# A written-out order of 1,538 steps replaced by one of 1,570, on a fused attention and filter kernel

## The chip, the cores and the metric

The kernel runs on one core of one Trainium2 chip. The metric is the device time of one execution in microseconds (us). Of the kernel before, three executions were timed: 292.82, 293.58 and 296.74 us, median 293.58 us. The profile is of one execution on that core.

The core has a matrix engine (PE, with its weight loads shown as PEld), a vector engine (DVE), a scalar engine (ACT), a general engine (POOL) and a sequencer for transfers (SP). Each engine works through its own list of instructions in order. POOL and SP also issue transfers: those of POOL run in one transfer queue (q0, "software_dynamic" in the profile), those of SP in another (q1, "hardware_dynamic").

## The reference

The computation is a feature-map attention for 8 batches and 8 heads over 576 positions, whose output goes through a gated circular convolution:

```python
def phi(x):
    proj = np.einsum('bhsd,df->bhsf', x, w_phi)              # 64 -> 128 features
    proj = proj - np.max(np.abs(proj), axis=-1, keepdims=True)
    return np.concatenate([np.exp(proj), np.exp(-proj)], axis=-1)
q_p, k_p = phi(q), phi(k)
kv  = np.einsum('bhsf,bhsd->bhfd', k_p, v)
z   = np.sum(k_p, axis=2)
num = np.einsum('bhsf,bhfd->bhsd', q_p, kv)
den = np.einsum('bhsf,bhf->bhs', q_p, z)[..., None] + 1e-06
x   = (num / den).transpose(0, 2, 1, 3).reshape(8, 576, 512)

proj = x @ w_proj                                            # 512 -> 3 * 512
x1, x2, x3 = thirds of proj
x2_conv = irfft(rfft(x2, n=576) * rfft(filter, n=576), n=576)
out = (x1 * x2_conv * x3) @ w_out
```

Inputs and output are float32. q, k and v have the shape (8, 8, 576, 64), the output (8, 576, 512).

## The kernel before

**Stages.** Each of the eight batches b goes through the same chain. Its parts are named by short words, which are also the method names of the class `Kernel`:

- `load` and `loadh` (lines 596 and 602) fetch a batch, or half a batch, of q, k or v through POOL's queue as bf16. `trh` (line 608) transposes half a batch of q or k by a transfer that SP issues. For batch 0 the transposes run on PE instead (`pt`, line 618), with a copy out of PSUM (`pte`).
- `Pk`, `Qn` (and `Pkt`, `Qnt` for the leftover positions) multiply by w_phi on PE (lines 636, 643, 651). `maxk`, `maxq` take the maxima of the absolute values on DVE (line 716). `ex` takes the exponentials of k on ACT (line 698). `mhi`, `mlo`, `trm`, `trme` prepare the maxima of q as a transposed row, and `Pq` (lines 670 and 676) projects q with those maxima subtracted; `ex` takes its exponentials too.
- `em` (ACT, line 752) and `vs` (POOL, line 758) scale v. `KV` (line 773), `KVe`, `NE` (line 787), `rc` and `xn` (lines 801 and 806) make the normalised attention output. `trx` (line 825) transposes it by a transfer of SP, `ptx` on PE.
- `f1`, `f2` (lines 854 and 860, sums and differences, on POOL or DVE), `Ft` and `Fs` (PE, lines 869 and 876) are the forward transform; `Fe` and `Xl` copy it out. `X2` (line 895), `Y1` (lines 900 and 905, DVE) and `m3` (line 909) project and multiply by the filter's transform. `I` (line 970), `Ie` (ACT, line 988), `Ip`, `Im` (DVE, line 991) are the inverse transform. `X1`, `X3` (line 917), `X1e`, `tm` and `ym` (line 1005) give the gate, `O` (line 1016), `Oe` and `st` (line 1040) the output.

**Start.** The transform matrices are made on the chip: `gi_part`, `gi_col`, `gi_fr`, `gi_nr`, `gi_back` write index numbers on POOL (iota), `cols_a`, `cols_b` and `ang` make angles of them (DVE, one `ang` on ACT), `frac` takes them into range (DVE), `sin` takes sines (ACT). The filter is fetched by nine transfers of SP (`fl_loadt`, `fl_load`), `fa` (POOL, line 495) makes its sums and differences `fs`, then `rev`, `fb`, `Ff`, `Ffe`, `H` and `He` make its transform. `wz` multiplies zeros on PE and feeds nothing. `exz` loads ACT's table for exponentials.

**What sets the order.** Nothing is scheduled by a tool here. The string `PLAN` lists all steps, and `run` calls them one by one; the order in which the calls of one engine stand is that engine's list. A word such as `Pk,1,0@2` is the step, its arguments (batch, part) and its PSUM bank; `KVe,ACT,1,0@4` names the engine that does the copy. Buffers go round as `RING` says (line 22): a step that writes a buffer waits until its last reader is done.

**Space in the start.** `fs`, the filter's sums, lies in the tile `turn`, which also holds the angles. So `fa` waits until the sines have read them:

```python
self.fs = self.turn.rearrange("p a x -> p (a x)")[:, 0:2048].rearrange(
    "p (a x) -> p a x", a=4)
```

The index numbers `fr` and `nr` have tiles of their own.

Of the kernel before, what the change touches and what calls it, by code (L numbers as in the profile page):

```python
# [30 lines left out]
gz,DVE sin,9 fz,DVE cz,DVE,0 loadh,q,0,0 gi_nr cz,DVE,1 gi_part gi_col cols_a cols_b cols_h  # L31
loadh,k,0,0 gi_fr ang,DVE,2 wz,23@0 wz,30@1 wz,31@0 wz,32@1 wz,33@0 ang,ACT,3 fl_loadt ident frac,3
frac,2 pt,q,0,0,0@0 pt,q,0,0,1@1 ang,DVE,1 wz,0@2 wz,34@3 wz,35@2 pt,k,0,0,0@3 ang,DVE,0
pt,k,0,0,1@2 frac,1 pte,DVE,q,0,0,1@1 zeros frac,0 fl_load,0,0 fl_load,2,1 ft,DVE fl_load,0,1
w_load,phi w_phi gi_back wz,18@1 back pte,DVE,k,0,0,0@3 Pk,0,0@4 loadh,q,0,1 sin,3 pte,ACT,q,0,0,0@0
pte,DVE,k,0,0,1@2 loadh,k,0,1 sin,2 sin,1 one Qn,0,1@0 Pk,0,1@2 pt,q,0,1,0@6 wz,27@7 sin,0 wz,14@7
fl_load,1,1 pt,k,0,1,1@7 exz ex,k,m,0,1@2 maxk,0,0@4 maxq,0,1@0 fl_load,3,1 fl_load,2,0 ex,k,p,0,0@4
pt,k,0,1,0@0 load,v,0 ex,k,m,0,0@4 pt,q,0,1,1@1 load,k,1 fl_load,3,0 maxk,0,1@2 pte,ACT,k,0,1,1@7
fl_load,1,0 pte,DVE,q,0,1,0@6 pte,ACT,k,0,1,0@0 Qn,0,0@4 pte,ACT,q,0,1,1@1 load,q,1 fa,POOL,0
maxq,0,0@4 Pkt,0@6 Qn,0,3@0 trh,k,1,0 maxkt,0@6 ex,k,p,0,1@2 wz,24@4 wz,17@2 trh,q,1,0 Qnt,0@4  # L40
maxq,0,3@0 fa,POOL,1 em,p,0,0 exkt,p,0@6 Pk,0,2@0 exkt,m,0@6 Qn,0,2@2 ex,k,p,0,2@0 maxqt,0@4
Pk,0,3@6 maxq,0,2@2 em,m,0,0 ex,k,m,0,3@6 w_load,proj,2 mhi,0 ex,k,p,0,3@6 rev@4 maxk,0,2@0
vs,POOL,p,0,0 mlo,POOL,0 vs,POOL,m,0,0 ex,k,m,0,2@0 trm,0@2 trme,DVE,0@2 Pq,0,0@2 ex,q,p,0,0@2
Pq,0,1@0 maxk,0,3@6 fb,0@4 em,m,0,1 em,p,0,1 vs,POOL,p,0,1 fb,1@4 wz,11@6 wz,9@7 KV,0,0@6
ex,q,p,0,1@0 ex,q,m,0,1@0 ex,q,m,0,0@2 Pq,0,3@4 Pq,0,2@0 ex,q,m,0,3@4 KVe,DVE,0,0@6 vs,POOL,m,0,1
NE,0,0@6 rc,0,0@6 NE,0,1@2 xn,0,0@6 trh,q,1,1 ex,q,p,0,3@4 Ff,2@6 Pk,1,1@4 rc,0,1@2 xn,0,1@2
f1,POOL,0,0,0 maxk,1,1@4 ex,q,p,0,2@0 Ffe,ACT,2@6 KV,0,1@2 Qn,1,0@6 ex,q,m,0,2@0 wz,5@0
# [1049 lines left out]
```

## Time and profile before

| | us |
|---|---|
| median of three executions | 293.58 |
| span of the profiled execution | 291.2 |
| PE busy | 274.0 (94%) |
| DVE busy | 252.3 (87%) |
| POOL busy | 228.5 (78%) |
| ACT busy | 221.9 (76%) |
| transfers: q1 (SP) / q0 (POOL), share of 16 transfer engines | 48.0% / 36.6% |

For the profiled execution the span, from the first to the last instruction, is the time that is given; the median of the timed executions is 2.4 us more. Busy time counts each matmul with its whole passage, and matmuls overlap, so a PE that is shown as busy need not be at its highest pace. "Idle before" in a row is the time in which the engine stood still ahead of that instruction, with what ended it.

### The profile page before, as it was taken

The numbers are of one execution on the slowest core, as the hardware profiler recorded it, in microseconds if no ns is written. First come the engines' busy times: TensorE is split into PE (matmuls) and PEld (weight loads), VectorE is DVE, ScalarE is ACT, GpSimd is POOL, SyncE is SP. The second block draws the span as 40 slices with busy tenths as digits, with TensorE's granted clock in tenths as the row PEclk, the third lists the DMA queues.
The fourth block names the chain that finished last, engine by engine and source line by source line (L and its number), as shares of the span: only waits on it lengthen the run. The fifth ranks groups of instructions, "written<-read, shape, count | busy, mean of one in ns | idle before, by whom it ended". The sixth has DMA issues, their size and how long they took to land.

```text
span 291.2 us, 10275 instructions
## 1 busy us (share of the span) xinstructions
PE 274.0 (94%) x4336; PEld 194.8 (67%) x4336; DVE 252.3 (87%) x438; ACT 221.9 (76%) x367; POOL 228.5 (78%) x187
## 2 busy tenths in 40 slices
...
GB/s 140 230 207 175 144 204 165 139 175 181 143 192 177 163 204 159 153 119 165 122 111 156 197 169 114 163 135 191 99 14 93 84 36 2 34 108 54 69 130 184
DMA packets 72319, 40.07 MB, mean 138 GB/s; under 512 B 52496, under 2 KB 67216, under 8 KB 72272
## 3 DMA queue, kind: packets, MB, share of 16 engines
q1 hardware_dynamic: 57136, 22.62, 48.0%
q0 software_dynamic: 14816, 16.25, 36.6%
...
q10 hardware_dynamic: 320, 0.52, 0.7%
q14 instruction: 13, 0.11, 0.1%
HBM read 33.75 MB, written 9.44 MB: 148 GB/s over the span
## 4 chain that ended last, share of the span: by engine, by line
PE 71%; DVE 3%; ACT 2%; issue 1%; DVEq 0%; ACTq 0%
PE ps L917 17%; PE ps L895 11%; PE ps L1016 10%; PE ps L970 8%; PE ps L773 5%; PE ps L787 4%; PE ps L876 3%; PE ps L926 2%; PE ps L670 2%; PE ps L636 2%; PE ps L643 2%; PE ps L676 2%; PE ps L869 2%; DVE mq L716 1%; PE ps L796 1%
## 5 line engine op out<-in xcount | busy, mean ns | idle before, releaser
L917 PE MATMUL ps<-xT,wproj 128*128 128x256 bf16 x512 | 64.0, 273 | 0.2 <-DMA wproj<-in_moe_w_proj_dram 0.2
L917 PEld LDWEIGHTS <-wproj 128*128 128x128 bf16 x512 | 48.1, 98 | 9.0 <-DMA wproj<-in_moe_w_proj_dram 0.4
L1005 POOL TENSOR_TENSOR yT<-cv,x1s 128x576 bf16<-128x576 f32 x31 | 39.4, 1279 | 15.6 <-ACT es L988 7.7
L716 DVE TENSOR_REDUCE mq<-ps 128x8 f32<-128x1024 f32 (+1 forms) x40 | 43.7, 1112 | 3.5 <-PE ps L643 1.5
L716 DVE TENSOR_REDUCE mk<-ps 128x8 f32<-128x1024 f32 (+1 forms) x40 | 44.1, 1112 | 2.9 <-PE ps L636 1.6
L758 POOL TENSOR_TENSOR vm<-vn,vm 128x1152 bf16<-128x1152 bf16 x16 | 34.3, 2152 | 7.4 <-ACT vm L752 7.4
L758 POOL TENSOR_TENSOR vp<-vn,vp 128x1152 bf16<-128x1152 bf16 x16 | 34.4, 2155 | 4.6 <-ACT vp L752 4.5
L698 ACT ACTIVATE Eqp<-ps 128x1024 bf16<-128x1024 f32 x32 | 32.9, 1038 | 6.1 <-PE ps L676 6.0
L854 POOL TENSOR_TENSOR SD<-xn 128x512 bf16<-128x512 bf16 x28 | 31.9, 1153 | 6.2 <-DVE xn L806 4.7
L1016 PE MATMUL ps<-wout,yT 128*128 128x512 bf16 x140 | 34.8, 379 | 0.1
L860 POOL TENSOR_TENSOR xf<-SD 128x512 bf16<-128x512 bf16 x26 | 29.7, 1155 | 6.4 <-DVE SD L854 5.9
L698 ACT ACTIVATE Ekp<-ps 128x1024 bf16<-128x1024 f32 x32 | 33.2, 1036 | 1.1 <-PE ps L636 0.7
L698 ACT ACTIVATE Eqm<-ps 128x1024 bf16<-128x1024 f32 x32 | 32.6, 1037 | 1.6 <-PE ps L676 0.8
L698 ACT ACTIVATE Ekm<-ps 128x1024 bf16<-128x1024 f32 x32 | 33.1, 1033 | 0.8 <-PE ps L636 0.7
L895 PE MATMUL ps<-wproj,XF 128*128 128x512 bf16 x128 | 31.6, 379 | 0.3 <-ACT x1s L298 0.3
L991 DVE TENSOR_TENSOR cv<-es,ps 128x288 f32<-128x288 f32 x64 | 26.3, 445 | 5.7 <-ACT es L988 4.4
L909 POOL TENSOR_TENSOR T<-T,T 128x1024 bf16<-128x1024 bf16 x14 | 29.6, 2127 | 1.7 <-DVE r L801 0.8
L970 PE MATMUL ps<-inv,T 128*128 128x288 bf16 x192 | 28.1, 286 | 0.7 <-DVE mq L716 0.4
L958 DVE TENSOR_TENSOR x1s<-ps,x1s 128x512 bf16<-128x512 f32 x32 | 21.8, 685 | 2.5 <-PE ps L917 1.1
L298 ACT COPY o<-ps 128x512 f32<-128x512 f32 x20 | 11.8, 600 | 14.4 <-PE ps L1016 12.0
L806 DVE TENSOR_TENSOR xn<-ps,r 128x512 bf16<-128x512 f32 x32 | 21.9, 689 | 0.9
L298 ACT CAST x1s<-ps 128x512 bf16<-128x512 f32 (+1 forms) x33 | 17.4, 540 | 6.7 <-PE ps L917 3.2
...
## 6 DMA issues: line engine op xcount, KB each, us to landing
...
```

The costliest lines, as they stand in the source:

```text
L298: self.nc.scalar.copy(dst, src)
L698: self.nc.scalar.activation(e, p, AF.Exp, bias=0.0, scale=1.0 if g == "p" else -1.0)
L716: self.nc.vector.tensor_reduce(out=out, in_=src, axis=AX.X, op=ALU.max, apply_absolute_value=True)
L758: self.eng(eng).tensor_tensor(out=t[:, :, :, 0:64], in0=self.at("vn", b)[:, 2 * X:2 * X + 2], in1=t[:, :, :, 64:65].to_broadcast([128, 2, ...
L854: self.eng(eng).tensor_tensor(out=o[:, :, 2 * i:2 * i + 2, :], in0=x[:, :, 0:2, :], in1=x[:, :, 2:4, :], op=ALU.subtract if i else ALU.add)
L860: self.eng(eng).tensor_tensor(out=o[:, :, 2 * i:2 * i + 2, :], in0=x[:, :, 0:4:2, :], in1=x[:, :, 1:4:2, :], op=ALU.subtract if i else ALU ...
L895: self.mm(self.pb(0), l, w[:, kt, 512:1024], start=(kt == 0), stop=(kt == 3))
L909: self.eng(eng).tensor_tensor(out=Y, in0=Y, in1=self.at(f"T{2 * e + 1}", b), op=ALU.add)
L917: self.mm(o[:, d], w[:, kt, f0 + 128 * m:f0 + 128 * m + 128], y[:, 1, ::-1, ::-1] if d else y[:, 0], start=(kt == 0), stop=(kt == 3))
L970: self.mm(self.pb(e, 0, 288), l, inv[:, 2 * e + i if i < 2 else 4 + e, :], start=(i == 0), stop=(i == 2))
L1005: self.eng(eng).tensor_tensor(out=self.at("yT", b)[:, m, 0:SEQ], in0=self.turn_of("cv", (b, m)).rearrange("p x h t -> p (x h t)"), in1=sel ...
L1016: self.mm(self.pb(0), y[:, kt, 128 * c:128 * c + 128], w[:, kt, :], start=(kt == 0), stop=(kt == 3))
```

## The change

Four things change.

1. **The table of steps.** All of `PLAN` is replaced. The steps are the same apart from the inverse transform (point 4), but they stand in another order, with other PSUM banks, and some are given to another engine:

| step | before | after |
|---|---|---|
| `Fe` | 25 ACT, 7 DVE | 22 ACT, 10 DVE |
| `Ffe` | 4 ACT | 2 ACT, 2 DVE |
| `Xl` | 7 ACT, 1 DVE | 1 ACT, 7 DVE |
| `Oe` | 20 ACT, 15 DVE | 24 ACT, 11 DVE |
| `X1e` and `X1te` | 33 ACT, 7 DVE | 31 ACT, 9 DVE |
| `pte` | 4 ACT, 4 DVE | 2 ACT, 6 DVE |
| `yt` | 3 ACT, 1 DVE | 2 ACT, 2 DVE |
| `m3` | 14 POOL, 2 DVE | 12 POOL, 4 DVE |
| `ym` | 31 POOL, 1 DVE | 29 POOL, 3 DVE |
| `f2` | 26 POOL, 6 DVE | 24 POOL, 8 DVE |

`f1`, `KVe`, `trme`, `ptxe` and `He` keep their counts but change places: two `f1` of batch 1 go from POOL to DVE, and two of batch 5 go back.

2. **Index steps first.** In POOL's list the index steps stand ahead of the first `loadh`, and the first load is of k, where it was of q.

POOL's first instructions before, from the end of the program's prologue to the second load (nr, part, idx and raw are index numbers, qn and kn the inputs q and k of batch 0):

```order
L602 DMA qn_76<-in_q_dram 128x2x576
L342 ISA
L342 IOTA nr 128x256
L344 IOTA nr 128x32
L322 IOTA part 128x1
L323 IOTA idx 128x128
L388 IOTA raw 128x4
L389 IOTA raw 128x1
L390 MEMSET raw 1x1
L602 DMA kn_78<-in_k_dram 128x2x576
```

The same place after, to the first load (fsx is the new tile, which now holds fr and nr):

```order
L319 IOTA part 128x1
L320 IOTA idx 128x128
L385 IOTA raw 128x4
L386 IOTA raw 128x1
L387 MEMSET raw 1x1
L329 IOTA fsx 128x288
L330 IOTA fsx 128x2x16
L332 IOTA fsx 128x2x128
L334 MEMSET fsx 128x1
L339 IOTA fsx 128x256
L341 IOTA fsx 128x32
L599 DMA kn_78<-in_k_dram 128x2x576
```

Eleven index instructions now stand ahead of the first load, the four on `fr` among them, which came behind the second load.

3. **Filter sums in their own space.** A new tile `fsx` holds `fs`; `fr` and `nr` lie in its first 864 columns. `turn` holds angles alone. `fa` so waits for the readers of `fr` and `nr`, no longer for the sines.

POOL's list around `fa` before (line 495; vn is v, mh the prepared maxima of q, wproj the projection's weights):

```order
L596 DMA vn_80<-in_v_dram 128x4x576
L596 DMA kn_79<-in_k_dram 128x4x576
L596 DMA qn_77<-in_q_dram 128x4x576
L495 TENSOR_TENSOR turn<-fl 128x1024 x2
L586 DMA wproj_65<-in_moe_w_proj_dram 128x4x512
L758 TENSOR_TENSOR vp_105<-vn_80,vp_105 128x18x64
L740 TENSOR_TENSOR mh_90<-mq_88,mh_90 128x2x18
```

And after (line 492):

```order
L593 DMA vn_80<-in_v_dram 128x4x576
L593 DMA kn_79<-in_k_dram 128x4x576
L492 TENSOR_TENSOR fsx<-fl 128x1024 x2
L593 DMA qn_77<-in_q_dram 128x4x576
L755 TENSOR_TENSOR vp_105<-vn_80,vp_105 128x18x64
L737 TENSOR_TENSOR mh_90<-mq_88,mh_90 128x2x18
L755 TENSOR_TENSOR vm_119<-vn_80,vm_119 128x18x64
```

The load of q of batch 1 moved from ahead of the two sums to behind them, and the first weight load of `w_proj` left this place for one further on.

DVE's list before, at its first reductions (kT and qT are the transposed inputs, mk and mq the maxima):

```order
L593 CAST wphi_62<-phi 128x128
L501 TENSOR_SCALAR bk<-idx_277 128x128
L300 COPY kT_84<-ps 128x640
L300 COPY kT_84<-ps 128x512
L353 TENSOR_TENSOR onex<-ident_63 128x36
L354 SCALAR_TENSOR_TENSOR one_64<-onex 128x18
L716 TENSOR_REDUCE mk_86<-ps 128x2x4
L716 TENSOR_REDUCE mq_88<-ps 128x2x4
L716 TENSOR_REDUCE mk_86<-ps 128x2x4
L300 COPY qT_82<-ps 128x640
L716 TENSOR_REDUCE mq_88<-ps 128x2x4
```

And after:

```order
L590 CAST wphi_62<-phi 128x128
L498 TENSOR_SCALAR bk<-idx_258 128x128
L297 COPY kT_84<-ps 128x512
L713 TENSOR_REDUCE mk_86<-ps 128x2x4
L297 COPY qT_82<-ps 128x640
L297 COPY qT_82<-ps 128x512
L305 MEMSET mh_90 128x64
L305 MEMSET mh_91 128x64
L713 TENSOR_REDUCE mk_86<-ps 128x2x4
L297 COPY kT_84<-ps 128x512
L713 TENSOR_REDUCE mq_88<-ps 128x2x4
```

One copy stands ahead of the first reduction now, where two copies and the two instructions of `one` did; further copies come between the reductions.

4. **Inverse leftovers apart.** `I` (six matmuls, each over 128 rows) is gone. In its place stand `Is` (four matmuls, the main rows) and one of two forms for the leftover rows: `It` (two matmuls over 64 rows each, 15 times) or `Iz` (two matmuls over 128 rows, 17 times). Main and leftover rows may come in either order: `opens` remembers which of the two was called first, and that one starts the sum in PSUM. `Ft` and `Fs` are handled in the same way.

The last lines of the two tables, and the code:

```diff
-Oh,7,4,0@5 Oh,7,4,1@7 st,SP,7,2,1 st,ACT,7,0,0 Oeh,DVE,7,4,0@5 sth,SP,7,4,0 Oeh,DVE,7,4,1@7
-sth,SP,7,4,1
+sth,SP,7,4,0 st,ACT,7,1,1 Oh,7,4,1@2 Oe,DVE,7,2@4 st,SP,7,2,1 Oeh,DVE,7,4,1@2 st,SP,7,0,1 sth,SP,7,4,1
+st,ACT,7,2,0
...
     def gi_fr(self):
-        g, s = self.nc.gpsimd, self.scr
-        self.fr = s.tile([128, 2, 2, 144], FP32, name="fr")
+        g = self.nc.gpsimd
+        self.fr = self.fsx[:, 0:576].rearrange("p (a b x) -> p a b x", a=2, b=2)
...
     def gi_nr(self):
-        g, s = self.nc.gpsimd, self.scr
-        self.nr = s.tile([128, 288], FP32, name="nr")
+        g = self.nc.gpsimd
+        self.nr = self.fsx[:, 576:864]
...
+    def opens(self, *key):
+        new = key not in self.opened
+        self.opened.add(key)
+        return new
...
     def Fs(self, b, v):
         xf, D = self.at("xf", b), self.at("D")
+        new = self.opens("F", b, v)
         for e in range(2):
             for s in range(2):
                 self.mm(self.pb(e, 144 * s, 144 * s + 144), xf[:, v, 2 * s + e, :],
-                        D[:, 288 * e + 144 * s:288 * e + 144 * s + 144], start=False,
-                        stop=(s == 1))
+                        D[:, 288 * e + 144 * s:288 * e + 144 * s + 144], start=new and s == 0,
+                        stop=not new and s == 1)
...
-    def I(self, b, m):
-        c, inv = slice(128 * m, 128 * m + 128), self.at("inv")
-        for e in range(2):
-            Y = self.at(f"T{2 * e}", b)
-            for i in range(3):
-                l = Y[:, i, c] if i < 2 else self.at("T4", b)[:, c]
-                self.mm(self.pb(e, 0, 288), l, inv[:, 2 * e + i if i < 2 else 4 + e, :],
-                        start=(i == 0), stop=(i == 2))
-
     def It(self, b, m):
-        c, inv = slice(128 * m, 128 * m + 128), self.at("inv")
+        c, inv, new = slice(128 * m, 128 * m + 128), self.at("inv"), self.opens("I", b, m)
         for e in range(2):
             r = slice(64 * e, 64 * e + 64)
-            self.mm(self.pb(e, 0, 288), self.at("T4", b)[r, c], inv[r, 4 + e, :], start=True,
-                    stop=False)
+            self.mm(self.pb(e, 0, 288), self.at("T4", b)[r, c], inv[r, 4 + e, :], start=new,
+                    stop=not new)
+
+    def Iz(self, b, m):
+        c, inv, new = slice(128 * m, 128 * m + 128), self.at("inv"), self.opens("I", b, m)
+        for e in range(2):
+            self.mm(self.pb(e, 0, 288), self.at("T4", b)[:, c], inv[:, 4 + e, :], start=new,
+                    stop=not new)
 
     def Is(self, b, m):
-        c, inv = slice(128 * m, 128 * m + 128), self.at("inv")
+        c, inv, new = slice(128 * m, 128 * m + 128), self.at("inv"), self.opens("I", b, m)
         for e in range(2):
             for i in range(2):
                 self.mm(self.pb(e, 0, 288), self.at(f"T{2 * e}", b)[:, i, c],
-                        inv[:, 2 * e + i, :], start=False, stop=(i == 1))
+                        inv[:, 2 * e + i, :], start=new and i == 0, stop=not new and i == 1)
...
-        self.fs = self.turn.rearrange("p a x -> p (a x)")[:, 0:2048].rearrange(
-            "p (a x) -> p a x", a=4)
+        self.fsx = s.tile([128, 2048], FP32, name="fsx")
+        self.fs = self.fsx.rearrange("p (a x) -> p a x", a=4)
```

More of the change, by code (lines that the diff above doesn't have):

```diff
@@ L30 @@
 PLAN = """
[L31 to L47, printed above, removed]
-KVe,ACT,0,1@2 ex,k,m,1,1@4 Pk,1,0@2 maxq,1,0@6 ex,k,p,1,1@4 maxk,1,0@2 NE,0,3@0 rc,0,3@0 Ff,3@6
@@ L193 @@
[L193 to L198 removed]
+fl_loadt gi_part gi_col gz,DVE wz,27@3 wz,14@3 wz,33@1 gi_fr wz,35@7 sin,9 fz,DVE fl_load,3,1
```

313 lines of the change are left out of this document (164 added, 149 removed).

## The prediction

> **What bounds the kernel now.** I read the page first, then the busy time of each engine by stretch, then what PE waited for, then the start in order of time.
>
> ```profile
> span 291.2 us, 10275 instructions
> PE 274.0 (94%) x4336; PEld 194.8 (67%) x4336; DVE 252.3 (87%) x438; ACT 221.9 (76%) x367; POOL 228.5 (78%) x187
> ```
>
> PE stands first, DVE second. These are averages over unlike stages, so the stretches decide (columns: stretch and its length; busy us and instructions of PE, PEld, DVE, ACT, POOL; granted clock, transfer share, GB/s):
>
> ```profile
> 0.00:20.00 20.00, 13.80 (x134) 6.81 (x134) 17.12 (x71) 15.42 (x25) 14.25 (x27) 1.00 1.01 191
> 20.00:85.00 65.00, 60.51 (x1123) 43.89 (x1120) 59.18 (x89) 60.74 (x99) 54.44 (x44) 1.00 1.19 169
> 85.00:215.00 130.00, 129.98 (x2110) 93.87 (x2107) 116.60 (x176) 103.19 (x172) 115.63 (x87) 1.00 0.97 149
> 215.00:245.00 30.00, 29.07 (x442) 21.05 (x439) 27.58 (x47) 25.66 (x42) 23.07 (x17) 1.00 0.28 52
> 245.00:292.00 47.00, 40.66 (x542) 29.21 (x540) 31.79 (x59) 16.92 (x31) 21.08 (x16) 0.97 0.40 90
> ```
>
> From 85 to 215 us PE hardly pauses (0.02 us), and DVE has 13.4 us to spare. From 20 to 85 us nobody has much: ACT is idle for 4.3 us, DVE for 5.8, PE for 4.5. From 215 to 245 us PE pauses for 0.9 us and DVE for 2.4. In the first 20 us, work waits for inputs:
>
> ```profile
> PE ps L618 <- DMA qn<-in_q_dram: 1.9, 2, 1.1
> PE ps L618 <- DMA kn<-in_k_dram: 1.8, 2, 1.5
> PE ps L917 <- DMA wproj<-in_moe_w_proj_dram: 0.2, 1, 0.2
> ```
>
> These are all the transfers that PE was seen to wait for, 3.9 us in sum. So an order that treats the two transfer queues better can win this and what hangs on it, and the rest must come from the engines.
>
> **The start (term A).** Rows of the timeline (start, length, instruction):
>
> ```profile
> 1.25 0.89 POOL L602 DMA_DIRECT2D qn<-in_q_dram  x1 [0.80 <-POOLq L1081]
> 2.23 0.40 POOL L342 IOTA nr<- 128x256 f32 x1
> 3.15 0.16 DVE L394 SCALAR_TENSOR_TENSOR raw<-raw,cols 128x2 f32<-128x2 f32 x1 [0.63 <-POOL raw L388]
> 3.22 0.76 POOL L602 DMA_DIRECT2D kn<-in_k_dram  x1
> 4.92 0.24 POOL L327 IOTA idx<- 128x128 f32 x1
> 6.79 0.68 PE L618 MATMUL ps<-ident,qn 128*128 128x128 bf16 x9 [1.14 <-DMA qn<-in_q_dram]
> 7.08 0.68 ACT L473 ACTIVATE inv<-turn 128x576 bf16<-128x576 int32 x1 [0.95 <-DVE turn L453]
> 7.67 0.94 ACT L475 ACTIVATE inv<-turn,cols 128x288 bf16<-128x288 int32 x2
> 8.07 0.76 POOL L596 DMA_DIRECT2D qn<-in_q_dram  x1
> 10.24 0.68 PE L618 MATMUL ps<-ident,kn 128*128 128x128 bf16 x9 [1.49 <-DMA kn<-in_k_dram]
> 11.34 1.28 ACT L701 ACT_TABLE_LOAD   x1
> 12.14 1.22 DVE L716 TENSOR_REDUCE mk<-ps 128x8 f32<-128x1024 f32 x1
> 12.74 1.01 ACT L698 ACTIVATE Ekm<-ps 128x1024 bf16<-128x1024 f32 x1
> 13.36 4.65 POOL L495 TENSOR_TENSOR turn<-fl 128x1024 f32<-128x1024 f32 x2 [4.53 <-ACT ez L701]
> 23.56 1.04 ACT L698 ACTIVATE Eqp<-ps 128x1024 bf16<-128x1024 f32 x1
> ```
>
> The index instructions ran in two pieces, 2.23 to 3.22 us and, behind the load of k (0.76 long), 3.98 to 4.92 us: 1.9 us together. Started at about 0.8 us (the wait ahead of the first load), they end near 2.7 us, and the first load (now k) goes out there, 1.5 us later than the first load before, but 0.5 us earlier than the load of k. The first load took 5.5 us from issue to its first matmul (1.25 to 6.79), so k can be transposed at about 8.2 us, where it was 10.24. Its maximum is then held not by k but by DVE's chain of angles. That chain waited for raw until 3.15 us; raw is now among POOL's first instructions, ready near 1.5 us. The chain gains some 1.5 us, so the first reduction falls near 10.7 instead of 12.14 us. What eats the gain: DVE now has two more copies of transposed blocks between the reductions (0.42 us each, as a row of 512 bf16 columns below). On ACT the copy of k stands ahead of two sines. It ends near 8.9 us; the last angles are ready about 9.4; sines of 0.68 + 0.94 and 0.68, the table load (1.28) and ez (0.2) bring the first exponential to 13.2 us, 0.5 later than before. Behind it ACT is spared two copies of about 0.63 us. I take the first exponential of q (23.56) 0.5 us earlier; the ends are 1.5 earlier (DVE's whole gain) and 1.5 later (the whole delay of the first load, if it lands late).
>
> Here the Trainium skill speaks against the change: "DMA: Bandwidth & Descriptors", section "Queues, rings and completion order", says that each transfer engine takes whole packets in turn from the queues that have work. By it the filter's queue keeps its turns while k is fetched, and a load issued 1.5 us later ends 1.5 us later or more; term A would be +1.5 us by the page alone. That is the late end above.
>
> The sums of the filter lose their wait for ez (13.36 us), but still wait for the last filter piece. The load of q of batch 1 stands behind them now, some 9 us later in POOL's list (8.07 before). The transfers of its queue ahead of it cover this, since they run until it would have its turn; if that cover fails, its transposes come late by as much as q's last reader in batch 1 has no other work, 1 us at most. The first gate projection stays where it is:
>
> ```profile
> 31.25 0.81 POOL L586 DMA_DIRECT2D wproj<-in_moe_w_proj_dram  x1
> 39.49 1.05 PE L917 MATMUL ps<-xT,wproj 128*128 128x256 bf16 x8 [0.22 <-DMA wproj<-in_moe_w_proj_dram]
> ```
>
> This load stands behind four products with v and one `f1` in both lists, and it lands 8.2 us after issue. An earlier start is not carried past 39 us by more than the 0.2 us of this wait and what POOL runs ahead.
>
> **The moved copies (term B, 20 to 85 us).** Prices from the groups by line and shape (busy us, mean ns):
>
> ```profile
> L298 ACT CAST XF<-ps 128x576 bf16<-128x576 f32 x25 | 15.2, 644 | 7.6 <-PE ps L876 7.6
> L300 DVE CAST XF<-ps 128x576 bf16<-128x576 f32 x7 | 5.2, 753 | 2.6 <-PE ps L876 2.6
> L298 ACT COPY XL<-XF 128x512 bf16<-128x512 bf16 x7 | 4.4, 630 | 1.3 <-DVE XF L300 1.2
> L300 DVE COPY XL<-XF 128x512 bf16<-128x512 bf16 x1 | 0.3, 283 | 0.0
> L298 ACT COPY o<-ps 128x512 f32<-128x512 f32 x20 | 11.8, 600 | 14.4 <-PE ps L1016 12.0 <-DMA out_dram<-o 2.3
> L300 DVE COPY o<-ps 128x512 f32<-128x512 f32 x15 | 10.3, 685 | 3.3 <-PE ps L1016 3.2
> L909 POOL TENSOR_TENSOR T<-T,T 128x1024 bf16<-128x1024 bf16 x14 | 29.6, 2127 | 1.7 <-DVE r L801 0.8 <-DVE T L905 0.8
> L909 DVE TENSOR_TENSOR T<-T,T 128x1024 bf16<-128x1024 bf16 x2 | 1.3, 683 | 0.0
> L860 POOL TENSOR_TENSOR xf<-SD 128x512 bf16<-128x512 bf16 x26 | 29.7, 1155 | 6.4 <-DVE SD L854 5.9
> L860 DVE TENSOR_TENSOR xf<-SD 128x512 bf16<-128x512 bf16 x6 | 2.3, 416 | 0.0
> ```
>
> In this stretch DVE takes two `Ffe` and one `Fe` (3 x 0.75), one `Oe` (0.69), one `Xl` (0.28) and, net, one of `f1` and `f2` (0.42), and gives one `KVe` (about 0.70, as an o of nearly the same columns) and one small copy (0.2) away: +2.7 us. ACT loses three copies of 0.64, one of 0.60 and one of 0.63 and takes 0.61 and 0.3: -2.2 us. POOL loses one 1.16. So DVE goes from 59.2 to 61.9 us and ACT from 60.7 to 58.5: the fuller engine of the two has 1.2 us more than before. If the stretch is as long as its fullest engine plus the 4.3 us that this engine is idle now, it grows by 1.2 us. If it follows ACT alone, it shrinks by 2.2; if DVE keeps its 5.8 us of idle time, it grows by 2.7. I take +0.5, since both lie within 1.6 us of each other now and work for both is at hand.
>
> **The inverse transform (term C).** PE's work is the same but for 15 `It`. In the chain of waits twelve matmuls of `I` took 1.47 us, 0.12 each:
>
> ```profile
> 274.45 1.47 PE ps L970 x12
> 258.24 0.42 PE L869 MATMUL ps<-Dt,xnt 64*128 64x288 bf16 x4
> 258.59 0.67 PE L876 MATMUL ps<-D,xf 128*128 128x144 bf16 x8
> ```
>
> An `It` is two matmuls over half the rows. The nearest row is `Ft`: four such matmuls, in two pairs that run beside each other, and the next line starts 0.35 us after them (258.24 to 258.59), where two times 0.12 would be 0.24. So a pair costs 0.12 and the change back to full rows 0.11: an `It` takes 0.23 us where `Iz` takes 0.24. Fifteen give 0.2 us, with ends of 0 and 15 x 0.12 = 1.8 us. I take 0.3, near the row.
>
> The Trainium skill, "TensorEngine Tiling (Array Packing)", has both sides: up to twofold speed for a contraction over at most 64 rows ("Theoretical Speedup"), and a drain of the array at each change of tiling ("Key Properties"). By the speedup alone the sum would have -1.8 us here, by the drain about none; the trace bears out the drain with its 0.11 us.
>
> **The rest.** From 85 to 215 us the further moves to DVE are a few us against 13.4 us of idle time behind a PE that does not pause: nothing, as long as PE's next operand is not the one moved; uncovered, they cost their own length. From 215 to 245 us one `f2` leaves POOL (1.16) for DVE (0.42), and PE has 0.9 us of pauses: -0.5 (term D; -0.9 to +0.4). At the end the order of the last six output blocks differs, but the last one is still a half block copied by DVE and sent by SP: 0, between -1 and +1.
>
> Sum: -0.5 + 0.5 - 0.3 - 0.5 = -0.8 us on the span, 290.4 us. The median of the timed runs lies 2.4 us above the span, so 292.8 us.
>
> **The rivals.**
>
> *ACT was the limit (faster).* ACT gives up 7 us in all (6 `Xl` x 0.63, 3 `Fe` and 2 `Ffe` x 0.64, and others, less 4 `Oe` x 0.60). If the crowded stretch follows ACT, B is -2.2; with A at -1.5, C at -1.8 and D at -0.9 the sum is -6.4: 287.2 us. For it: ACT is the fullest engine from 20 to 85 us. Against it: DVE is 1.6 us behind it there. Chance 0.17.
>
> *DVE becomes the limit (slower).* All moves together give DVE 5 x 0.75 (`Fe`, `Ffe`), 6 x 0.28, 2 x 0.68 (`m3`), 2 x 0.42, two `ym` (0.75, as 576 columns of XF), two `pte` (0.42), one `X1e` (0.69), one `X1te` (0.4, half as wide) and one `yt` (0.2), less 4 `Oe` x 0.69: +8.5 us. If its 39 us of idle time are waits that the order cannot fill, the kernel grows by all of this: 293.6 + 8.5 = 302.1 us. It decides where DVE's share reaches that of PE, which from 20 to 85 us is nearly so (59.2 against 60.5) and later not. Chance 0.11.
>
> *The late first load.* Term A at +1.5, and again as much where ACT's sines stand behind the copy of k: 295 to 296.6 us. For it: k's copy stands ahead of two sines on ACT. Against: DVE's angles end later than k lands. Chance 0.14.
>
> *The queue order does nothing.* PE's waits for transfers are 3.9 us, all but 0.2 in the first 15 us, and the engines beside it are busy by then: 293.6 us. Chance 0.10.
>
> The forecast itself has the remaining 0.48.
>
> **How the numbers follow.** The predicted time is 292.8 us. The range runs from 287.0, which takes in the first rival's sum, to 299.0 us, which takes in the late load and more than half of DVE's 8.5 us; outside are about 0.08 below and 0.11 above. A difference of 2% is 5.9 us, about what a measurement of this kernel tells from no change. Faster than that (under 287.7): 0.6 of the first rival and a little of the forecast, 0.12. Slower (over 299.5): 0.8 of the second rival and a little of the others, 0.11. Within: 0.77.
>
> **What would show it.** In the profile after: the load of k issued near 2.7 us and its transposes near 8.2; the first reduction near 10.7, the first exponential near 13.2, that of q near 23.1 us; the first gate projection still near 39 us; DVE busy about 261 us, ACT 215, POOL 219; PE busy for nearly all of 85 to 215 us. Wrong I would be if PE waits for a transposing transfer in the middle (none is seen now), if `It` starts much sooner after itself than 0.23 us, or if DVE's idle time stays at 39 us with the longer list.

## The result: slower by 9%

The changed kernel took 322.05 us (median of four executions, 319.02 to 328.59) where the kernel before took 293.58 beside it. The ratio is 1.091, with a 95% interval of 1.083 to 1.100. The profiled execution took 319.02 us, its span is 317.2. For the experiments below, go by the ratios: they leave out the executions that ran some per cent longer at a lower granted clock, and the medians do not.

The page of the changed kernel (span; busy time of the engines; granted clock of PE in 40 slices):

```profile
span 317.2 us, 10240 instructions
PE 279.0 (88%) x4305; PEld 197.1 (62%) x4336; DVE 280.7 (88%) x456; ACT 219.1 (69%) x355; POOL 221.0 (70%) x181
PEclk9997999999999996999997998999999999999999
```

ACT and POOL are near the prediction (215 and 219 us). DVE was to have 261 us and has 280.7, which is 28.4 more than before. The granted clock has holes in four slices. By stretches (columns as in the prediction):

```profile
0.00:20.00 20.00, 14.43 (x138) 7.60 (x140) 17.05 (x66) 15.42 (x24) 12.38 (x26) 1.00 0.95 182
20.00:85.00 65.00, 56.91 (x1063) 41.14 (x1062) 62.01 (x93) 56.14 (x91) 53.15 (x43) 0.97 1.14 159
85.00:215.00 130.00, 114.50 (x1807) 82.03 (x1821) 114.02 (x159) 86.62 (x138) 95.84 (x73) 0.95 0.87 133
215.00:245.00 30.00, 29.25 (x396) 20.96 (x399) 28.64 (x42) 21.53 (x40) 23.41 (x16) 1.00 0.64 121
```

From 85 to 215 us, where PE had not paused, it is now without work for 15.5 us (130 less 114.50). What it waited for (total, times, longest):

```profile
PE ps L784 <- DVE KVs L297: 4.4, 1, 4.4
PE ps L921 <- DMA xT<-xn: 4.2, 3, 2.6
PE ps L880 <- DVE xf L857: 3.4, 1, 3.4
PE ps L673 <- DVE one L351: 1.8, 1, 1.8
PE ps L872 <- DVE x1s L297: 1.7, 1, 1.7
```

Four of the five are DVE's, one is a transposing transfer. DVE's groups by shape (busy us, mean ns) say why DVE is late:

```profile
L857 DVE TENSOR_TENSOR xf<-SD 128x512 bf16<-128x512 bf16 x8 | 11.7, 1464 | 0.6 <-POOL SD L851 0.6
L913 DVE TENSOR_TENSOR T<-T,T 128x1024 bf16<-128x1024 bf16 x4 | 9.0, 2259 | 0.0
L297 DVE COPY XL<-XF 128x512 bf16<-128x512 bf16 x7 | 5.6, 806 | 0.1
L851 DVE TENSOR_TENSOR SD<-xn 128x512 bf16<-128x512 bf16 x4 | 2.8, 699 | 0.0
L1006 DVE TENSOR_TENSOR yT<-cv,x1s 128x576 bf16<-128x576 f32 x3 | 3.3, 1107 | 0.1
L909 DVE TENSOR_TENSOR T<-ps,HTe 128x1024 bf16<-128x1024 f32 x16 | 19.1, 1216 | 0.2
```

The same instructions were shorter before: `xf` 416 ns, `T<-T,T` 683 and `XL` 283 (rows in the prediction), and in the kernel before also:

```profile
L854 DVE TENSOR_TENSOR SD<-xn 128x512 bf16<-128x512 bf16 x4 | 1.7, 417 | 0.1
L1005 DVE TENSOR_TENSOR yT<-cv,x1s 128x576 bf16<-128x576 f32 x1 | 0.8, 759 | 0.0
L905 DVE TENSOR_TENSOR T<-ps,HTe 128x1024 bf16<-128x1024 f32 x16 | 19.2, 1217 | 0.2
```

The excess is 8 x 1048 + 4 x 1576 + 7 x 523 + 4 x 282 + 3 x 348 ns = 20.5 us, and one `onex` adds 1.95. These forms have one thing in common: all their inputs lie in SBUF. The last row of each list reads PSUM (`ps`), and it is as long as before, 1216 ns against 1217. So most of the 28.4 us is not the added work but the same work made longer. Two instances show how. DVE, POOL and PE around 116 us:

```profile
116.61 5.73 DVE L857 TENSOR_TENSOR xf<-SD 128x512 bf16<-128x512 bf16 x1
122.26 0.68 DVE L962 TENSOR_TENSOR x1s<-ps,x1s 128x512 bf16<-128x512 f32 x1
```

```profile
115.69 2.16 POOL L755 TENSOR_TENSOR vp<-vn,vp 128x1152 bf16<-128x1152 bf16 x1
117.80 2.15 POOL L755 TENSOR_TENSOR vm<-vn,vm 128x1152 bf16<-128x1152 bf16 x1
119.90 2.15 POOL L755 TENSOR_TENSOR vp<-vn,vp 128x1152 bf16<-128x1152 bf16 x1
```

```profile
117.95 1.03 PE L1017 MATMUL ps<-wout,yT 128*128 128x512 bf16 x4
122.39 0.66 PE L880 MATMUL ps<-D,xf 128*128 128x144 bf16 x4 [3.41 <-DVE xf L857]
```

This is `f2,DVE,2,1,0`. POOL ends its third product at 122.05 us, and `xf` ends 0.29 us later (116.61 + 5.73 = 122.34). It stood still through all of POOL's work, and PE behind it. At 163.76 us `m3,DVE,3,0` did the same for 5.43 us, with the copy of KVs behind it in DVE's list, for which PE waited 4.4 us:

```profile
163.76 5.43 DVE L913 TENSOR_TENSOR T<-T,T 128x1024 bf16<-128x1024 bf16 x1
169.11 0.68 DVE L297 CAST KVs<-ps 128x520 bf16<-128x520 f32 x1
```

Twelve steps are stretched like this, each beside POOL's arithmetic. In the kernel before, 17 instructions on DVE read SBUF alone behind the making of the transform matrices (from 11.86 us on). Not one of them ran beside arithmetic on POOL, so its rows show them all at their shortest.

Behind the stop at 119 us PE is slow as well (stretch and length; PE, PEld, DVE, ACT, POOL; clock):

```profile
120.00:122.00 2.00, 0.00 (x0) 0.00 (x0) 2.00 (x1) 0.00 (x0) 2.00 (x1) 0.82 0.97 189
122.00:124.00 2.00, 1.33 (x12) 0.73 (x12) 2.00 (x4) 0.00 (x0) 0.05 (x1) 0.50 0.08 19
126.00:128.00 2.00, 1.78 (x20) 1.12 (x18) 1.43 (x2) 2.00 (x3) 2.00 (x2) 0.50 0.51 107
128.00:130.00 2.00, 2.00 (x14) 1.25 (x13) 1.34 (x2) 1.69 (x2) 0.14 (x1) 0.97 0.77 96
```

From 124 to 126 us the clock is 0.50 too, so some 7 us run at half clock. Behind the stop at 165.5 us it is 3.4 us.

### The profile page after: what moved, and what is told of

Its sections match the earlier page's. It is cut to its first block, busy times and chain, and to the rows that moved or that the text cites. A ratio compares the mean times of both kernels' runs of the same rounds, so it can differ in the third digit from the quotient of the medians.

```text
span 317.2 us, 10240 instructions
## 1 busy us (share of the span) xinstructions
PE 279.0 (88%) x4305; PEld 197.1 (62%) x4336; DVE 280.7 (88%) x456; ACT 219.1 (69%) x355; POOL 221.0 (70%) x181
## 4 chain that ended last, share of the span: by engine, by line
PE 53%; DVE 24%; DMA 9%; issue 7%; ACT 4%; POOL 1%; SPq 1%; DVEq 0%; ACTq 0%
PE ps L921 12%; PE ps L899 9%; PE ps L1017 5%; DVE mq L713 5%; DVE mk L713 4%; PE ps L784 4%; PE ps L770 4%; PE ps L985 4%; DMA kT<-kn 4%; DMA xT<-xn 3%; PE ps L930 2%; PE ps L880 2%; DMA phi<-in_w_phi_dram 2%; DVE T L909 2%; DVE cv L992 2%
## 5 line engine op out<-in xcount | busy, mean ns | idle before, releaser
L921 PE MATMUL ps<-xT,wproj 128*128 128x256 bf16 x512 | 67.3, 279 | 4.8 <-DMA xT<-xn 4.2
L921 PEld LDWEIGHTS <-wproj 128*128 128x128 bf16 x512 | 48.9, 99 | 16.4 <-issue 6.3
L1006 POOL TENSOR_TENSOR yT<-cv,x1s 128x576 bf16<-128x576 f32 x29 | 37.2, 1297 | 22.7 <-DVE cv L992 16.6
L1017 PE MATMUL ps<-wout,yT 128*128 128x512 bf16 x127 | 33.9, 380 | 0.8
L913 POOL TENSOR_TENSOR T<-T,T 128x1024 bf16<-128x1024 bf16 x12 | 25.5, 2125 | 12.0 <-DVE T L909 11.9
L899 PE MATMUL ps<-wproj,XF 128*128 128x512 bf16 x116 | 30.6, 382 | 1.4 <-issue 0.7
L857 POOL TENSOR_TENSOR xf<-SD 128x512 bf16<-128x512 bf16 x24 | 27.6, 1162 | 0.9 <-DVE SD L851 0.5
L295 ACT CAST x1s<-ps 128x512 bf16<-128x512 f32 (+1 forms) x31 | 16.8, 542 | 12.2 <-PE ps L921 9.5
L784 PE MATMUL ps<-KVs,Eqp 128*128 128x65 bf16 x256 | 19.9, 194 | 5.4 <-DVE KVs L297 4.4
L295 ACT COPY o<-ps 128x512 f32<-128x512 f32 x24 | 14.0, 592 | 13.2 <-PE ps L1017 13.2
L295 ACT CAST XF<-ps 128x576 bf16<-128x576 f32 x22 | 13.6, 642 | 13.2 <-PE ps L872 9.0
```

Source lines behind the costliest of these rows:

```text
L295: self.nc.scalar.copy(dst, src)
L784: self.mm(self.pb(u, 65 * a, 65 * a + 65), E, KVs[:, u, v, s, :], start=(s == 0), stop=(s == 1))
L857: self.eng(eng).tensor_tensor(out=o[:, :, 2 * i:2 * i + 2, :], in0=x[:, :, 0:4:2, :], in1=x[:, :, 1:4:2, :], op=ALU.subtract if i else ALU ...
L899: self.mm(self.pb(0), l, w[:, kt, 512:1024], start=(kt == 0), stop=(kt == 3))
L921: self.mm(o[:, d], w[:, kt, f0 + 128 * m:f0 + 128 * m + 128], y[:, 1, ::-1, ::-1] if d else y[:, 0], start=(kt == 0), stop=(kt == 3))
L1006: self.eng(eng).tensor_tensor(out=self.at("yT", b)[:, m, 0:SEQ], in0=self.turn_of("cv", (b, m)).rearrange("p x h t -> p (x h t)"), in1=sel ...
```

## The experiments

Three theories stood against each other. The first: DVE stands still while POOL reads SBUF, and the change put DVE's steps there. The second: the order of loads and transposing transfers costs the time. The third: the new order as a whole keeps DVE behind. The place where the time goes is read from one step's end, the reciprocal `rc,b,0` of each batch, in each profile (us later than in the kernel before, whose times are in the first row):

| kernel | ratio (95%) | b=0 | 1 | 2 | 3 | 4 | 5 | 6 | 7 |
|---|---|---|---|---|---|---|---|---|---|
| before, at us | 1 | 28.5 | 65.7 | 88.1 | 124.1 | 152.5 | 183.0 | 226.0 | 251.1 |
| changed | 1.091 (1.083-1.100) | 1.7 | 2.9 | 5.2 | 13.4 | 18.7 | 24.9 | 25.2 | 24.9 |
| old order, new code | 1.000 (0.997-1.004) | -0.1 | -0.3 | -0.3 | -0.2 | 0.0 | 0.1 | 0.5 | 0.5 |
| before, nine steps to DVE | 1.049 (1.039-1.058) | -0.1 | -0.2 | 0.6 | 9.8 | 10.0 | 10.2 | 12.6 | 14.2 |
| before, one word | 1.030 (1.025-1.034) | 0.5 | 0.4 | 0.3 | 9.4 | 9.5 | 9.5 | 9.5 | 9.5 |
| the same, PE kept busy | 1.029 (1.020-1.039) | 0.5 | 0.3 | 0.3 | 7.5 | 9.1 | 9.1 | 10.0 | 10.0 |
| changed, twelve steps mended | 1.080 (1.071-1.088) | 4.7 | 6.4 | 10.1 | 16.4 | 16.6 | 22.5 | 24.3 | 24.4 |
| changed, four words | 1.053 (1.046-1.059) | 1.8 | 2.9 | 5.2 | 8.2 | 10.0 | 14.8 | 15.1 | 15.2 |
| changed, late load | 1.080 (1.072-1.088) | 1.7 | 3.4 | 7.0 | 16.1 | 21.6 | 23.3 | 23.6 | 23.7 |
| changed, eleven words | 1.040 (1.026-1.054) | 0.3 | 1.4 | 5.9 | 8.2 | 8.4 | 8.9 | 9.1 | 8.8 |
| changed, six words | 1.022 (1.013-1.031) | -0.2 | 1.3 | 3.5 | 6.4 | 6.6 | 7.1 | 7.4 | 7.6 |
| changed, 24 steps, `one`, late load | 1.028 (1.012-1.043) | -1.0 | 0.6 | 2.4 | 3.5 | 3.7 | 4.2 | 6.8 | 6.8 |

**The code alone.** The changed code with the old table; each `I` becomes two words:

```diff
-I,0,2@2
+Iz,0,2@2 Is,0,2@2
```

> The changed code (filter sums in their own space, inverse as two steps) with the order of the kernel before; each I is written as Iz, Is, so that the same matmuls run with the zero half. All three theories say that the code itself costs nothing: 293 to 294.5 us. Were the code the cause (a wait on fsx, the split accumulation of the inverse), it would come out at 300 us or more.

It took 294.25 us, ratio 1.000. The separate space for the filter sums and the split inverse cost nothing and bring nothing. All of the 9% is in the table of steps.

**Twelve steps taken off DVE, in the changed order.**

```diff
-Xl,DVE,0  f1,DVE,1,0,0  f2,DVE,1,0,1  f2,DVE,1,1,1  f2,DVE,2,1,0  m3,DVE,3,0
+Xl,ACT,0  f1,POOL,1,0,0 f2,POOL,1,0,1 f2,POOL,1,1,1 f2,POOL,2,1,0 m3,POOL,3,0
-f2,DVE,5,0,1  ym,DVE,5,0  Xl,DVE,6 m3,DVE,6,0  Xl,DVE,7
+f2,POOL,5,0,1 ym,POOL,5,0 Xl,ACT,6 m3,POOL,6,0 Xl,ACT,7
+one
 load,v,0
...
-one
```

> The changed kernel with twelve steps whose inputs all lie in SBUF taken off VectorE's time beside GpSimd: four f2, one f1, two m3, one ym are given back to GpSimd (f2 1,0,1; 1,1,1; 2,1,0; 5,0,1; f1 1,0,0; m3 3,0 and 6,0; ym 5,0), three Xl to ScalarE (0, 6, 7), and one moved ahead of the first load of v, all otherwise in the changed order. Theory 1 (VectorE stands still while GpSimd reads SBUF, whenever its own operation has two SBUF inputs or is a bf16 copy): VectorE's busy time falls from 280.7 us by their 26 us to 252 to 258 us, the PE waits on KVs (4.4 us), xf (3.4), one (1.8) and x1s (1.7) go, and the time falls from 322.0 to 300 to 310 us. Theory 2 (the order of the transposing transfers and loads is what costs): VectorE's busy time falls by the same steps' counted 6 us only, the waits for xT and kT stay, and the time stays within 3 us of 322. Theory 3 (the new order as a whole keeps VectorE too far behind PE): about 318 us, since 6 us of 281 come off VectorE.

318.11 us: the number of the third theory, not of the first. DVE's busy time fell to 267.4 us, neither to 252-258 nor by 6 alone. Its profile tells why this was no clean test:

```profile
169.77 4.00 DVE L303 COPY XL<-XF 128x512 bf16<-128x512 bf16 x1
```

`Xl,DVE,3` took 0.28 us in the changed kernel. Here it has come to stand beside POOL's product and sum, and takes 4.0; `Xl,DVE,2` takes 3.39. The `onex` that was moved forward met the filter sums on POOL (2.29 us at 16.42 us), and PE stood still for 2.75 us behind it. What was taken away came back at other steps beside POOL's work.

**The same steps put into the kernel before.** Nine words of the old table, each where it stands:

```diff
-f1,POOL,1,0,0 f2,POOL,1,0,1 f2,POOL,2,1,0 m3,POOL,3,0 f2,POOL,5,0,1
+f1,DVE,1,0,0  f2,DVE,1,0,1  f2,DVE,2,1,0  m3,DVE,3,0  f2,DVE,5,0,1
-ym,POOL,5,0 Xl,ACT,6 m3,POOL,6,0 Xl,ACT,7
+ym,DVE,5,0  Xl,DVE,6 m3,DVE,6,0  Xl,DVE,7
```

> The kernel before, its order untouched, with nine of the same steps put on VectorE where they stand (f1 1,0,0; f2 1,0,1; 2,1,0; 5,0,1; m3 3,0 and 6,0; ym 5,0; Xl 6 and 7). By the rows they cost VectorE 4.6 us alone. Theory 1: those that meet a GpSimd operation take 1 to 5 us each, VectorE's busy time rises from 252.3 by 10 to 25 us, and the time rises from 293.6 to 299 to 308 us. Theories 2 and 3: VectorE's busy time rises by 4.6 us to 257, and the time stays at 293 to 296 us.

307.66 us, ratio 1.049, so some 14 us slower, at the upper end of the first theory; DVE's busy time rose by 12.2 us to 264.5. The old order has neither the new transfers nor the new sequence, so these nine words do it by themselves. The table of delays shows 9 of the 14 us between batches 2 and 3, where one step, `f2,2,1,0`, took 6.2 us.

**One word.** So that word was changed alone:

```diff
-f2,POOL,2,1,0
+f2,DVE,2,1,0
```

> The kernel before with one word changed: f2 2,1,0 on VectorE and not on GpSimd. Theory 1 with the clock: it starts at about 109 us beside GpSimd's f2, em and scaling steps, takes about 6 us and not 0.42, PE stops for 5.9 us and runs at half clock for some 7 us, and the time rises by 8.5 to 10 us to 303 to 305 us. By the counted price (0.42 us on VectorE, covered): 294 to 295 us. Were it the sum of the nine steps and not this one that made 307.7 us, it would be 295 to 298 us.

302.67 us, ratio 1.030, just under the first case and far from the second. The instruction, POOL beside it, and PE's wait:

```profile
109.11 6.21 DVE L860 TENSOR_TENSOR xf<-SD 128x512 bf16<-128x512 bf16 x1
115.24 0.68 DVE L300 COPY o<-ps 128x512 f32<-128x512 f32 x1
```

```profile
109.68 1.15 POOL L860 TENSOR_TENSOR xf<-SD 128x512 bf16<-128x512 bf16 x1
110.80 2.14 POOL L758 TENSOR_TENSOR vp<-vn,vp 128x1152 bf16<-128x1152 bf16 x1
112.90 2.14 POOL L758 TENSOR_TENSOR vm<-vn,vm 128x1152 bf16<-128x1152 bf16 x1
```

```profile
PE ps L917 <- DVE o L300: 5.7, 1, 5.7
```

A step of 0.42 us, moved from POOL to DVE, lasts until 0.28 us after POOL's last instruction (112.90 + 2.14 = 115.04; 115.32). PE waited 5.7 us not for its result but for a copy queued behind it on DVE. The delay of 9.5 us is complete by batch 3 and never made up.

**The clock's share.** 5.7 us of waiting became 9. To see whether the half clock makes the difference, 26 dummy matmuls into an unused bank fill the stop:

```diff
-f2,POOL,2,1,0
+f2,DVE,2,1,0
...
+wz,40@1 wz,41@1 wz,42@1 wz,43@1 wz,44@1 wz,45@1 wz,46@1
+wz,47@1 wz,48@1 wz,49@1 wz,50@1 wz,51@1 wz,52@1
 X3,2,0@0
```

> The kernel before with the one word changed (f2 2,1,0 on VectorE) and 26 dummy matmuls of 128 x 512, some 5.6 us in all, on TensorE in the place where it then stood still for 5.9 us, in a bank that nobody uses there; the outputs are untouched. If the stop costs by the clock too, the granted clock stays at 1.00 behind it, and the time falls from 302.7 to 299 to 300.5 us. If the half clock has another cause, or if PE makes up for it behind: 302 to 303.5 us.

The clock stayed up. One stretch behind the stop, first without the dummies, then with them:

```profile
116.00:118.00 2.00, 2.00 (x12) 1.51 (x12) 0.71 (x2) 0.00 (x0) 0.00 (x0) 0.50 0.97 195
116.00:118.00 2.00, 2.00 (x17) 1.33 (x16) 1.26 (x2) 0.66 (x2) 0.00 (x0) 1.00 1.27 271
```

The time did not fall: 304.29 us, ratio 1.029 where it was 1.030. The interval of 1.020 to 1.039 leaves room for some 3 us either way, so the steps have to tell. The copy of `KVs` of batch 3 that comes first behind the stop, in the kernel before, with the one word, and with the dummies too:

```profile
118.24 0.59 ACT L298 CAST KVs<-ps 128x520 bf16<-128x520 f32 x1 [0.25 <-PE ps L773]
126.70 0.59 ACT L298 CAST KVs<-ps 128x520 bf16<-128x520 f32 x1 [0.25 <-PE ps L773]
124.45 0.59 ACT L299 CAST KVs<-ps 128x520 bf16<-128x520 f32 x1 [0.25 <-PE ps L774]
```

Both kernels leave the stop 5.9 us late. At full clock this step comes 2.25 us earlier, so the half clock did cost time, as the first case said. The gain went again behind it, because PE stood still twice more. In the kernel with dummies, from 110 to 140 us:

```profile
PE ps L971 <- issue: 1.3, 1, 1.3
PE ps L774 <- issue: 1.2, 1, 1.2
```

"issue" is idle time in which PE waited for nothing that the profile shows. The delay grows there from 6.2 to 7.5 us, and from 7.6 to 9.1. The kernel without dummies has one such stop, of 0.8 us, where its delay grows from 8.5 to 9.4 us. POOL did not take the time: its sum `T<-T,T` of 120.82 us in the kernel before comes 4.1 us late with the dummies, 2.1 us less than PE. Each of the three stops begins within 0.5 us of the landing of a 16 KB transfer of the instruction queue (q8), which would fit a PE that waits for its own instructions; no run tests that. So of the 9.4 us at `rc,3,0` with the one word, 0.3 were there before the stop, some 5.6 are the stop itself, 2.6 come while PE runs at half clock, and 0.9 in the stop without a seen cause.

**Four words mended in the changed kernel.**

```diff
-f2,DVE,2,1,0  m3,DVE,3,0  Xl,DVE,2 Xl,DVE,3
+f2,POOL,2,1,0 m3,POOL,3,0 Xl,ACT,2 Xl,ACT,3
```

> The changed kernel with four steps taken off VectorE: f2 2,1,0 and m3 3,0 (the two that took 5.73 and 5.43 us, and behind which PE stood still for 3.6 and 4.5 us) back to GpSimd, Xl 2 and Xl 3 to ScalarE so that these do not meet GpSimd in their place. Theory 1, with the clock (a stop of PE of over about 3.5 us is followed by some 7 us at half clock, as in the kernel with nine steps moved): each stop cost its own length and 3 to 4 us more, and the time falls from 322 to 307 to 312 us. Theory 1 without the clock: 313 to 315 us. Theory 3 (the order keeps VectorE behind, and the next late step takes the place): 318 to 322 us, as when twelve steps were taken off.

309.69 us: 12.4 us less in the medians, 11 by the ratios. That is the first theory with the clock's price, and not without it. The delay at batch 3 falls from 13.4 to 8.2 us, that at batch 5 from 24.9 to 14.8. The third theory's number, 318 to 322, did not come.

**The transfers.** PE's 4.2 us for `xT` lie at 187 to 190 us. First the transfer waited for was issued earlier, behind the step that writes its rows:

```diff
+trx,4,3
 st,SP,2,3,1
...
-trx,4,3
```

> The changed kernel with one transposing transfer (trx 4,3, for which PE waits 2.7 us at 189.6 us) issued right behind the step that writes its rows, ahead of two stores and two other transfers, at about 177.3 us and not at 182.5. Theory 2: that wait goes, and the time falls by 2.5 to 4 us to 318 to 319.5 us; the other transfers in that place are the next to be waited for, at most 1 us. Theory 1: PE then has less time behind it but VectorE's blocked steps set the end anyway, 321 to 322.5 us.

320.53 us (1.079, interval 1.066 to 1.091): the interval overlaps that of the changed kernel, so the time does not decide. In the profile PE still waits 4.8 us for `xT`, where the second theory had at most 1 us left. The place in the queue was not it. Then the load that runs beside the transfers was moved:

```diff
-load,v,6
...
+load,v,6
 mlo,POOL,5
```

> The changed kernel with one load (v of batch 6, issued at 180.6 us, 7.9 us to landing) moved behind the steps up to 190.8 us, so that it does not move its 576 KB beside the transposing transfers of batch 4. Theory 2 (the load delays the transfers): the 4.2 us that PE waits for xT at 186.8 and 189.7 us go, and the time falls to 317.5 to 319.5 us. If the transfers are slow because of the stores and of each other: 320.5 to 322.5 us.

316.95 us, 5.1 less than the changed kernel in the medians and 3.3 by the ratios, whose intervals overlap a little. No wait for `xT` is left in that place, and from batch 4 to 5 the delay grows by 1.7 us where it grew by 6.2. The transfers from issue to landing, first in the changed kernel, then with the late load:

```profile
DMA to landing us min/median/max: 2.4/5.0/7.1
```

```profile
DMA to landing us min/median/max: 2.4/2.5/3.9
```

So the second theory is right at one place: with the 576 KB load issued at 180.6 us the four transposing transfers of batch 4 took twice as long, 5.0 us against 2.5 in the median.

**24 SBUF-only steps off DVE.** 24 words, and `one` moved ahead of `zeros`. Four such steps of the last batch stay on DVE:

> The changed kernel with all 24 steps with SBUF inputs alone that VectorE does beside GpSimd (f1, f2, m3, ym to GpSimd; Xl and one yt to ScalarE) taken off, and one put ahead of zeros; the order is otherwise the changed one. VectorE's busy time falls from 280.7 to 250 to 255 us, GpSimd's rises from 221 to about 240. Theory 1: no VectorE operation of over twice its length alone is left; what remains over the kernel before are the waits for transposing transfers and loads, and the time is 300 to 308 us. Theory 3: 314 us or more, with PE waiting for GpSimd's steps or for VectorE at other places; the share of the order itself is then over half of the loss.

311.38 us, between the two cases; by the ratio, 1.048 (1.038 to 1.058), it is some 308 us, the end of the first. DVE's busy time fell to 255.9 us. `one`, in its new place, met the filter sums on POOL:

```profile
14.52 2.05 DVE L356 TENSOR_TENSOR onex<-ident 128x36 bf16<-128x36 bf16 x1
16.61 2.27 DVE L357 SCALAR_TENSOR_TENSOR one<-onex 128x18 bf16<-128x18 bf16 x1
```

0.34 us of work took 4.3 us, and the delay at batch 0 rose to 7.0 us. With `one` ahead of `w_phi`, and the late load:

> The kernel with all 24 steps off VectorE, with two more words moved: one (4.3 us at 14.5 us in that run, beside GpSimd's filter sums) ahead of w_phi, where VectorE waits for a load and GpSimd does no arithmetic, and the load of v of batch 6 behind the steps up to 190.8 us. Theory 1 with the clock and theory 2: the stop of 4.6 us at 15.7 us and the wait for xT go, and the time is 297 to 303 us; what is then left over the kernel before (3 to 9 us) is the order's own. If the order's own share is more (PE waiting for GpSimd, which has 10 us more work than in the kernel before): 304 to 308 us.

The median is 306.47 us (301.86 to 307.81), in the second case. The kernel before was slower beside it as well (median 296.49), and the ratio is 1.028 (1.012 to 1.043), so the time does not decide between the two. The profiled execution took 301.86 us. In it DVE is back at 251.3 us, and the two `T<-T,T` and one `yT` that it still does take 686 and 758 ns, their lengths alone. No such step is stretched any more, and `rc,7,0` is still 6.8 us late: these are not the price of DVE standing still beside POOL.

**Six words.** The four, `one` ahead of `w_phi`, and the late load:

> The changed kernel with six words mended: the four of the run before (f2 2,1,0, m3 3,0, Xl 2, Xl 3 off VectorE), one ahead of w_phi, and the late load of v of batch 6. The single gains, 12.4 us of the four words, 5.1 us of the load (4.2 us by the waits), about 2 us of one, add up to 302.5 to 304.5 us if they are of separate places. If the second half is bound by something else, 306 to 308 us.

302.23 us, ratio 1.022 (1.013 to 1.031), 0.3 us below the first case: the gains add up about as forecast. Six words of some 1,570 bring back 19.8 of the 28.5 us, and about three quarters of the loss by the ratios as well. The last run tried the two places that its profile named for the rest:

```diff
-f1,DVE,1,0,0  f1,DVE,1,1,1  f2,DVE,1,0,1  f2,DVE,1,1,1
+f1,POOL,1,0,0 f1,POOL,1,1,1 f2,POOL,1,0,1 f2,POOL,1,1,1
+load,q,2
 Pqt,0@4
```

> The run with six words mended, and five more: the four half and sum steps of batch 1 that VectorE does at 74 to 97 us (f1 1,0,0; f1 1,1,1; f2 1,0,1; f2 1,1,1; 5.3 us of VectorE's time with their standing still, in a stretch where the chain of waits is VectorE's alone and 6 us of the remaining 8 are lost) to GpSimd, and the load of q of batch 2 issued ahead of the half steps of batch 0, some 6 us earlier, so that it does not move its bytes beside the transposing transfers that PE waits 1.8 us for at 54.7 us. If these two places hold the rest: 297 to 299.5 us (span 295 to 297). If GpSimd becomes the one that PE waits for there (as at 86.4 us with all steps on it, 2.0 us), 299.5 to 302 us. No gain, 302 to 303 us, would say that the rest is spread over the order.

No gain: 304.91 us, ratio 1.040 (1.026 to 1.054). PE waited 1.7 us for an `xf` on POOL, and DVE met POOL at yet another step, behind which PE waited 2.4 us:

```profile
89.33 2.90 DVE L303 COPY XL<-XF 128x512 bf16<-128x512 bf16 x1
```

The last 8 us over the kernel before are therefore not settled. Most of the delay arises between batches 0 and 3 (-0.2 to 6.4 us with six words, -1.0 to 3.5 with the 24 steps off DVE). In the latter kernel PE stands still for 1.8 us at 52.4 us, waiting for a transposing transfer of k, and for 1.7 us at 84.7 us, waiting for POOL's `xf`. Together that is as much as the 3.4 us by which the delay grows from batch 0 to 2. No version beat the kernel before.

## Why the prediction was wrong

**The step that failed** is the one on the rest: "nothing, as long as PE's next operand is not the one moved; uncovered, they cost their own length", with the lengths from the rows of the kernel before, 416 ns for `xf` and 683 for `T<-T,T`. The second half failed, and the condition of the first did not hold. PE's next operand was the one moved (`xf`, 3.4 us), or it stood behind the moved one on DVE (`KVs`, 4.4 us). And uncovered, the steps did not cost their own length: they took 5.73 and 5.43 us. The runs put a price on it: one such word, in the old order, made the kernel 9 us slower (ratio 1.030), and taking four off DVE in the changed kernel brought 11 to 12 us back. The rows gave the price in POOL's absence, since the old order did these steps only where POOL did no arithmetic. That could have been read from the trace: the six `xf` of 416 ns on average all ran with POOL idle beside them.

The Trainium skill has the rule in "SBUF — State Buffer", section "Who interferes with whom": DVE's second SBUF port pair is GpSimd's only one, and it is held exclusively for a whole instruction. A DVE instruction with two SBUF inputs contends with a GpSimd instruction that reads SBUF; copies and casts can, in the fast modes; one with a single SBUF input outside those modes does not. The trace agrees in kind: `T<-ps,HTe` with one input in PSUM kept its 1216 ns, the two-input steps and the bf16 copy were stretched. The prediction weighed what the Trainium skill says on queues and on tiling, and left this section out. The Trainium skill also says that whoever starts first blocks the other, and the trace has a case of that too, DVE's `xf` ahead of POOL's:

```profile
219.03 0.43 DVE L857 TENSOR_TENSOR xf<-SD 128x512 bf16<-128x512 bf16 x1 [0.63 <-POOL SD L851]
```

```profile
219.08 1.39 POOL L857 TENSOR_TENSOR xf<-SD 128x512 bf16<-128x512 bf16 x1
```

Here DVE kept its 0.43 us, and POOL took 1.39 where its `xf` took 1.155 on average before.

**Right sign, wrong size and cause: the rival "DVE becomes the limit".** It priced the moves at 8.5 us of DVE's time, 302.1 us. The moved work itself did cost DVE no more than that: 28.4 us less the 22.5 of stretching leaves 5.9. The mechanism was not the added work.

**The start (term A): right up to the stretched step.** The load of k went out at 2.70 us (2.7 was said), k was transposed at 8.41 (8.2), the first reduction came at 10.97 (10.7), the first exponential at 13.00 (13.2). The first exponential of q came at 25.29, not 23.1: `onex`, 0.16 us before, took 2.11 us at 22.36 us beside POOL's product, and PE waited 1.8 us for `one`. With `one` moved, `rc,0,0` was 0.2 us ahead of the kernel before, where term A had -0.5. The first load took 5.7 us from issue to its first matmul (2.70 to 8.41) where the first load before took 5.5, so the late-load rival did not show. The load itself did end later than the first load before, by 1.6 us (8.41 against 6.79). That is near the 1.5 us or more which the prediction worked out from the packet turns of the Trainium skill ("DMA: Bandwidth & Descriptors", "Queues, rings and completion order"). It did not carry on to term A: the first reduction still came 1.2 us earlier than before.

**The crowded stretch (term B): too small.** It had +0.5 us from 20 to 85 us. DVE's busy time there came out as forecast (62.0 us, 61.9 said), but with some 4.5 us of stretching in it, and from `rc,0,0` to `rc,2,0` the delay grew from 1.7 to 5.2 us. Without any stretched step (the 24 steps off DVE) it still grew by 3.4 us. PE's waits for a transfer and for POOL are as long, and the term had neither; no run took both away, so this part of the cause is open.

**The inverse (term C): half right.** `It` is followed by the next step after 0.12 to 0.15 us where that one uses 64 rows too (with one exception, 0.24 us at 140.65 us), and after some 0.22 us where it uses 128:

```profile
146.41 0.30 PE L972 MATMUL ps<-inv,T 64*128 64x288 bf16 x2
146.55 0.39 PE L640 MATMUL ps<-wphi,qT 64*128 64x128 bf16 x8
```

```profile
71.22 0.30 PE L972 MATMUL ps<-inv,T 64*128 64x288 bf16 x2
71.45 0.54 PE L985 MATMUL ps<-inv,T 128*128 128x288 bf16 x3
```

The prediction took 0.23 for all fifteen, and its sign of being wrong, a next `It` much sooner than 0.23 us, did come. So the change back to full rows costs about 0.1 us, and only where it happens. Nine of the fifteen are followed early, which is worth 1.0 us at most (9 x 0.11); the term was no cause of the loss.

**The middle's transfers: the stated exception came true.** "Wrong I would be if PE waits for a transposing transfer in the middle": it did, for 4.2 us, and one load less beside them brought 3 to 5 us.

**The last stretches (term D and the end): within their bounds.** The delay stays between 24.9 and 25.2 us from batch 5 to 7, so the -0.5 of term D did not come, but 0 is inside its bounds. The whole span is 26.0 us longer, 1.1 more than at `rc,7,0`, at the edge of the +1 given for the end.

**The rival on ACT** fell: ACT gave up 2.8 us of its busy time (221.9 to 219.1), not 7, and the kernel got no faster by it.
